# Two FFN-only steps behind the third batch, its loads a step later, and the first output stores issued by SyncE

## The chip, the cores and the metric

One core of a Trainium2 chip. The metric is the time of one execution in microseconds (us) of device time. A core's five engines are called here as the profile calls them: PE is TensorE, ACT is ScalarE, DVE is VectorE, POOL is GpSimd, SP is SyncE. Batches and steps are counted from 0, so the "third batch" of the title is batch 2.

## The reference

Attention over 8 batches of 8 heads, 576 queries of width 64, with 16 extra "beacon" keys ahead of the causal ones; its result goes through a gated FFN.

```python
k_all = np.concatenate([beacon_k, k], axis=2)          # 16 + 576 keys
v_all = np.concatenate([beacon_v, v], axis=2)
scores = scale * np.matmul(q, k_all.transpose(0, 1, 3, 2))
scores = np.where(causal, -1000000000.0, scores)       # future keys; beacons are always seen
a = np.exp(scores - scores.max(-1, keepdims=True))
a /= a.sum(-1, keepdims=True) + 1e-09
x = np.matmul(a, v_all)          # -> (4608 tokens, 512)
gate = np.maximum(x @ w_gate, 0.0)                     # 512 -> 1536
out = gate * (x @ w_val) @ w_out                       # 1536 -> 512
```

## The kernel before

Everything is laid out by hand as a list of steps. A step holds a share of one batch's attention (scores on PE, exp on ScalarE, causal mask on GpSimd, value products on PE, normalisation on VectorE) and some FFN groups of tokens that are finished, so that PE has matmuls while the other engines work. An "up" group is 8 matmuls of 512 columns with a relu and a product; a "down" group is 12 matmuls, a copy and an output store. Integer quotas count groups, the others are us of PE time.

```python
    ALONE = ((0, 3, 3, 2), (4, 4))          # FFN-only steps behind batch 0 and behind batch 1
    ...
    plan = ([(0, i, 0) for i in range(7)]
            + [(None, 0, n) for n in ALONE[0]]
            + [(1, i, 1) for i in range(7)]
            + [(None, 0, n) for n in ALONE[1]]
            + [(2, i, n) for i, n in enumerate((2, 2, 1, 1, 1))]
            + [(b, i, 6.2) for b in range(3, B) for i in range(5)]
            + [(None, 0, 4.5)])
```

From batch 2 on, a batch is brought in by 15 tiles: a load on SyncE's queue, a cast to bf16 on GpSimd some steps later, and for q and k a transposing DMA, again on SyncE's queue, a step after the cast.

```python
        def load(self, x, t, held=False):
            ...
                nc.sync.dma_start(raw[p0:p1].rearrange("p (h d) -> p h d", d=D), ...)
        def turn(self, x, t):
            ...
            nc.sync.dma_start_transpose(dst[:, :, t * P:t * P + n], self.h.pop((x, t))[:n])

        def fetch(b, s0, late=1, held=False):
            at(s0, lambda: batches.update({b: Batch(b)}))
            for j, u in enumerate(LOADS):
                s = s0 + j // 3
                at(s, lambda u=u, h=held and j == 0: batches[b].load(*u, h))
                at(s + late, lambda u=u: batches[b].cast(*u, pool))
                if u[0] != "v":
                    at(s + late + 1, lambda u=u: batches[b].turn(*u))

        fetch(2, s2 + 1, 2, True)                        # s2: the first step of batch 1
        for b in range(3, B):                            # BASE[b]: the first step of batch b
            fetch(b, BASE[b] - (7 if b == 3 else 5), 2 if b == 3 else 1)
```

The store of a down group goes out on one of two queues. The first two FFN tiles (8 stores) use ScalarE's, at once behind the copy. All later ones are put on a list and go out on SyncE's queue at the start of the next step.

```python
                ob = pools["osb"].tile([P, d_model], FP32, name="ob")
                nc.scalar.copy(ob[:, n], o[:, n])
                store = lambda e, m=m, n=n, ob=ob: e.dma_start(out[m:m + P, n], ob[:, n])
                if self.m0 < 2 * M_TILE:
                    store(nc.scalar)
                else:
                    later_sp.append(lambda store=store: store(nc.sync))
    ...
        for s, (b, i, quota) in enumerate(plan):
            acts = later.pop(s, [])           # this step's loads, casts, transposes
            run_sp()                          # the stores on the list
            ...                               # scores, exp, values, FFN groups
            for act_ in acts + later_half.pop(s, []):
                act_()
```

## Time and profile before

| | |
|---|---|
| time before, first three runs | median 395.3 us (394.73 to 400.1) |
| span of the profiled run | 393.6 us |
| PE busy | 371.9 us, so 21.7 us idle |
| the worst stop | 4.15 us before batch 3's first scores, then 3.8 us at clock 0.57 |

The lines behind these figures stand in the prediction and are not shown twice. One listing that is not part of the profile helps to read them: the compiled instruction list of the kernel before, which names the semaphores that each instruction waits for. On ScalarE's and SyncE's queues (row, line, operation, waits):

```
ScalarE
73 L539 TensorCopy ob<-p 128x512 [waits PE_49]
74 L541 DMACopy out_dram<-ob 128x512 [waits DMAHW5_49,Activation_49]
75 L411 Activation e<-p 128x2x3x160 [waits PE_49,Pool_49]
SyncE
82 L250 DMACopy raw<-in_v_dram 128x8x64 [waits DMAHW5_49]
83 L250 DMACopy raw<-in_v_dram 128x8x64 [waits DMAHW6_49]
84 L250 DMACopy raw<-in_v_dram 80x8x64 [waits DMAHW7_49]
85 L275 DmaTransposeAnt kT<-half 128x4x128 [waits DMAHW0_49,Pool_49]
86 L275 DmaTransposeAnt qT<-half 128x4x128 [waits DMAHW1_49,Pool_49]
```

The DMAs of SyncE and ScalarE share eight semaphores, DMAHW0 to DMAHW7, dealt out in the order of the program, and each DMA waits for the one that had its semaphore before. So the fifth store (row 74, with DMAHW5) waits for the v load eight DMAs earlier (row 82, with DMAHW5), on the other queue. That is the wait that the prediction calls a bookkeeping dependence. Call this set the ring.

### The profile page before, as it was taken

Reading aid. Unit: us, or ns where it says so; the run is one execution under the profiler, and the core shown is the slowest. Engines: PE = TensorE matmul, PEld = TensorE weight load, DVE = VectorE, ACT = ScalarE, POOL = GpSimd, SP = SyncE. Lnnn points to the kernel's source line nnn. Section 1 sums busy time; section 2 is a strip of 40 time slices with the busy share of each in tenths; the row PEclk is TensorE's granted clock in tenths of the full one; section 3 lists DMA queues with packets and bytes.
Section 4 is the critical chain, followed back from the end, with each engine's and each line's share of the span. In section 5 each row is a group of like instructions: output and inputs, shape, how many; then the busy total and the mean of one; then the engine's idle time right before and its main releaser. Section 6 shows DMA issues by size and latency. Waiting matters only on the chain.

```text
span 393.6 us, 10209 instructions
## 1 busy us (share of the span) xinstructions
PE 371.9 (94%) x4297; PEld 190.1 (48%) x4297; DVE 198.3 (50%) x309; ACT 191.0 (49%) x272; POOL 123.3 (31%) x219
## 2 busy tenths in 40 slices
PE   6889998989959999999999999999999999999995
PEld 2564544434535555555555555455545544444443
DVE  4768566342633466336742675257525665412420
ACT  3783583238625654575347544655455513323321
POOL 1696654235531523242424252324320200000000
PEclk9999999999998999999999999999999999999999
DMA  7999999799698665597558854985310011002002
GB/s 208 220 213 181 192 198 230 159 194 190 137 193 190 151 127 108 134 208 152 108 134 185 160 115 125 198 139 123 87 55 2 2 56 53 2 36 74 0 28 85
DMA packets 149220, 50.70 MB, mean 129 GB/s; under 512 B 133680, under 2 KB 144688, under 8 KB 149168
## 3 DMA queue, kind: packets, MB, share of 16 engines
q1 hardware_dynamic: 138960, 42.91, 50.5%
q0 software_dynamic: 9056, 4.98, 9.4%
q10 hardware_dynamic: 1152, 2.10, 1.8%
q8 instruction: 35, 0.57, 0.7%
q14 instruction: 17, 0.14, 0.1%
HBM read 38.34 MB, written 9.44 MB: 121 GB/s over the span
## 4 chain that ended last, share of the span: by engine, by line
PE 70%; DMA 16%; SPq 3%; POOL 3%; DVE 2%; ACT 2%; issue 2%; ACTq 0%; DVEq 0%; POOLq 0%
PE p L536 20%; PE p L517 19%; PE p L526 19%; PE p L466 6%; DMA raw<-in_v_dram 4%; DMA wv<-in_moe_w_val_dram 4%; DMA raw<-in_q_dram 3%; DMA raw<-in_k_dram 2%; PE p L403 2%; ACT e L411 2%; DVE hT L528 2%; SPq L250 1%; DMA wide<-in_k_dram 1%; SPq L275 1%; DMA hwide<-in_k_dram 1%
## 5 line engine op out<-in xcount | busy, mean ns | idle before, releaser
L528 DVE TENSOR_TENSOR hT<-g,p 128x512 bf16<-128x512 f32 x89 | 60.7, 684 | 101.2 <-PE p L526 66.9
L419 POOL TENSOR_SCALAR_AFFINE_SELECT e<-e 128x512 bf16<-128x512 bf16 (+2 forms) x80 | 45.7, 592 | 158.8 <-ACT e L411 158.7
L526 PE MATMUL p<-xT,wv 128*128 128x512 bf16 x356 | 91.3, 379 | 0.4 <-ACT e L411 0.4
L517 PE MATMUL p<-xT,wg 128*128 128x512 bf16 x356 | 91.5, 379 | 0.2
L520 ACT ACTIVATE g<-p 128x512 f32<-128x512 f32 x89 | 52.8, 603 | 71.3 <-PE p L517 71.3
L536 PE MATMUL p<-wo,hT 128*128 128x512 bf16 (+1 forms) x396 | 85.5, 373 | 0.2 <-ACT e L411 0.2
L411 ACT ACTIVATE e<-p 128x1024 bf16<-128x1024 f32 (+2 forms) x84 | 75.1, 966 | 21.0 <-PE p L403 12.2
L479 DVE RECIPROCAL r<-p 128x256 f32<-128x256 f32 (+1 forms) x24 | 47.0, 1958 | 43.3 <-PE p L466 43.3
L526 PEld LDWEIGHTS <-wv 128*128 128x128 bf16 x432 | 42.0, 98 | 53.0 <-issue 1.8
L536 PEld LDWEIGHTS <-hT 128*128 128x128 bf16 x444 | 42.1, 98 | 48.2 <-issue 0.5
L517 PEld LDWEIGHTS <-wg 128*128 128x128 bf16 x432 | 40.3, 98 | 49.8 <-issue 3.2
L539 ACT COPY ob<-p 128x512 f32<-128x512 f32 (+1 forms) x33 | 18.9, 573 | 63.5 <-PE p L536 63.5
L270 POOL CAST half<-raw 128x512 bf16<-128x512 f32 (+2 forms) x60 | 35.4, 614 | 17.8 <-DMA raw<-in_q_dram 10.1
L466 PEld LDWEIGHTS <-v 128*32 128x32 bf16 (+1 forms) x1408 | 28.6, 99 | 11.0 <-issue 5.3
L403 PEld LDWEIGHTS <-kT 64*128 64x128 bf16 x704 | 21.0, 97 | 25.6 <-issue 21.1
L466 PE MATMUL p<-e,v 128*32 128x80 bf16 (+4 forms) x1056 | 30.2, 235 | 1.5 <-DVE hT L528 1.0
L411 ACT ACTIVATE e<-s 128x1024 bf16<-128x1024 f32 (+2 forms) x28 | 25.6, 966 | 8.3 <-PE s L403 4.8
L403 PE MATMUL p<-qT,kT 64*128 64x80 bf16 (+3 forms) x528 | 23.3, 230 | 4.8 <-ACT e L411 4.4
L265 POOL CAST v<-raw 128x512 bf16<-128x512 f32 (+1 forms) x38 | 24.0, 656 | 7.6 <-DMA raw<-in_v_dram 7.5
L466 PE MATMUL p<-e,ones 128*32 128x80 bf16 (+4 forms) x528 | 25.0, 234 | 0.0
L517 PE MATMUL f<-xT,wg 128*128 128x512 bf16 x76 | 19.7, 379 | 2.0 <-ACT g L520 1.7
L466 PEld LDWEIGHTS <-ones 128*32 128x32 bf16 (+1 forms) x704 | 19.7, 100 | 0.1
(83 smaller groups left out, 228.3 us busy)
## 6 DMA issues: line engine op xcount, KB each, us to landing
out_dram<-ob SPq DMA_DIRECT2D x27, 256.0 KB, 2.2
raw<-in_q_dram SPq DMA_DIRECT2D x25, 256.0 KB, 5.0
raw<-in_v_dram SPq DMA_DIRECT2D x24, 256.0 KB, 4.1
raw<-in_k_dram SPq DMA_DIRECT2D x19, 256.0 KB, 5.0
out_dram<-ob ACTq DMA_DIRECT2D x8, 256.0 KB, 3.1
raw<-in_v_dram SPq DMA_DIRECT2D x8, 224.0 KB, 3.6
wo<-in_moe_w_out_dram POOLq DMA_DIRECT2D x2, 768.0 KB, 11.9
raw<-in_k_dram SPq DMA_DIRECT2D x6, 224.0 KB, 4.6
```

The costliest lines, as they stand in the source:

```text
L265: copy(self.v[:n, t].rearrange("p (h a d) -> p h a d", a=2, d=C), raw[:n].rearrange("p (h d a) -> p h a d", a=2, d=C))
L270: copy(h[:n], raw[:n])
L403: nc.tensor.matmul(self.s[:, a, c + j * n:c + (j + 1) * n], kT[rows, 2 * g + j, k0:k0 + P], qT[rows, 2 * g + j, q0:q0 + n], start=True, st ...
L411: nc.scalar.activation(e[:, :k * 4 * n].rearrange("p (k a x) -> p a k x", k=k, a=2), self.s[:, :, :k * 2 * n].rearrange("p a (k x) -> p a ...
L419: nc.gpsimd.affine_select(out=cols[:, :, :m], in_=cols[:, :, :m], pattern=[[0, 4], [1, m]], compare_op=ALU.is_ge, fill=0.0, base=base, cha ...
L466: nc.tensor.matmul(o[:, q0 - cq0:q0 - cq0 + n], w, e[:kr, 2 * (hh % 2) + hh // 2], start=(x == 0 and i == 0 and part != 1), stop=stop, ski ...
L479: nc.vector.reciprocal(self.r[:, :self.n], self.os[:, :self.n])
L517: nc.tensor.matmul(g[:, :n], wg[:, ki, nf * P:(nf + 1) * P], x[:, ki], start=(ki == 0), stop=(ki == KM - 1))
L520: nc.scalar.activation(gs[:, :n], g[:, :n], AF.Relu)
L526: nc.tensor.matmul(u[:, :n], wv[:, ki, nf * P:(nf + 1) * P], x[:, ki], start=(ki == 0), stop=(ki == KM - 1))
L528: nc.vector.tensor_mul(self.h[:, nf, c0:c1], gs[:, :n], u[:, :n])
L536: nc.tensor.matmul(o[:, n], self.h[:, nf, ms * P:(ms + 1) * P], wo[:, nf, n], start=(nf == 0), stop=(nf == NF - 1))
```

## The change

Its intent: SyncE is one to two steps late at batches 2 and 3, and its lateness reaches PE in two ways, through the transposed tiles and through ScalarE's queue. The change gives batch 3 more time (part B: two FFN-only steps in front of it, paid for by its own quota), lets batch 2's loads start a step later (part C, whose casts stay two steps behind), and takes the stores off ScalarE (part A), behind each step's loads and transposes.

```diff
-                store = lambda e, m=m, n=n, ob=ob: e.dma_start(out[m:m + P, n], ob[:, n])     # A
-                if self.m0 < 2 * M_TILE:
-                    store(nc.scalar)
-                else:
-                    later_sp.append(lambda store=store: store(nc.sync))
+                later_sp.append(
+                    lambda m=m, n=n, ob=ob: nc.sync.dma_start(out[m:m + P, n], ob[:, n]))
 ...
-    ALONE = ((0, 3, 3, 2), (4, 4))
+    ALONE = ((0, 3, 3, 2), (4, 4), (2, 3))                                                    # B
 ...
-            + [(b, i, 6.2) for b in range(3, B) for i in range(5)]
+            + [(None, 0, n) for n in ALONE[2]]
+            + [(b, i, 4.1 if b == 3 else 6.2) for b in range(3, B) for i in range(5)]
 ...
-        fetch(2, s2 + 1, 2, True)
+        fetch(2, s2 + 2, 2, True)                                                             # C
 ...
             acts = later.pop(s, [])
+            behind_acts = later_sp[:] if s < BASE[3] else []                                  # A
+            if behind_acts:
+                later_sp.clear()
             run_sp()
 ...
-            for act_ in acts + later_half.pop(s, []):
+            for act_ in acts + later_half.pop(s, []) + behind_acts:
                 act_()
```

(One effect of B is not in the diff's text: BASE[3] grows by two, so batch 3's loads are planned for step 20 and not 18.)

## The prediction

> **What bounds the kernel now.** I read the page first: the engine totals and the row of forty slices.
>
> ```profile
> span 393.6 us, 10209 instructions
> ...
> PE 371.9 (94%) x4297; PEld 190.1 (48%) x4297; DVE 198.3 (50%) x309; ACT 191.0 (49%) x272; POOL 123.3 (31%) x219
> ...
> PE   6889998989959999999999999999999999999995
> ...
> PEclk9999999999998999999999999999999999999999
> ```
>
> TensorE is the bound: it is idle for only 393.6 - 371.9 = 21.7 us. The change adds and removes no matmul, so it can win only idle time, and time in which the clock was low. One slice in the middle stands out (the twelfth, a 5), and the clock dips right after it. Then I took busy times by stretches. From 60 to 131 us PE is busy 62.19 of 71.0 us (8.8 idle); from 131 to 389 us it is busy 256.55 of 258 (1.45 idle in all). The rest of the idle time, some 11.5 us, lies before 60 us and in the last 5 us, where the diff changes nothing. So the whole prize is in 60 to 131 us. Around the bad slice the columns are window, length, busy time of PE, PEld, DVE, ACT, POOL, granted clock, DMA share, GB/s:
>
> ```profile
> 109.34:112.10 2.76, 2.76 (x20) 1.08 (x12) 2.60 (x3) 0.00 (x0) 1.07 (x2) 1.00 1.40 118
> 112.10:116.26 4.16, 0.01 (x2) 0.09 (x2) 0.51 (x2) 1.02 (x2) 0.00 (x0) 1.00 1.06 195
> 116.26:120.08 3.82, 3.47 (x96) 2.60 (x96) 0.10 (x1) 2.09 (x4) 2.23 (x4) 0.57 0.74 194
> ```
>
> A stop of 4.16 us, then 3.82 us at a clock of 0.57. The timeline of PE (start, length, what; in brackets the idle time before it and its releaser) shows what ended this stop, and an earlier one:
>
> ```profile
> 80.62 1.02 PE L517 MATMUL f<-xT,wg 128*128 128x512 bf16 x4 [1.69 <-ACT g L520]
> ...
> 116.26 0.40 PE L403 MATMUL p<-qT,kT 64*128 64x256 bf16 x4 [4.15 <-ACT e L411]
> ```
>
> Both times ScalarE was late, though it is busy only half the time. Its own timeline says why:
>
> ```profile
> 79.53 0.34 ACTq L541 DMA_DIRECT2D out_dram<-ob  x1
> 79.97 1.08 ACT L520 ACTIVATE g<-f 128x512 f32<-128x512 f32 x2 [3.87 <-DMA raw<-in_v_dram]
> ...
> 107.62 0.59 ACT L539 COPY ob<-p 128x512 f32<-128x512 f32 x1 [2.05 <-PE p L536]
> 114.79 0.34 ACTq L541 DMA_DIRECT2D out_dram<-ob  x1
> 115.23 1.56 ACT L411 ACTIVATE e<-p 128x960 bf16<-128x960 f32 x2 [7.03 <-DMA raw<-in_v_dram]
> ```
>
> ScalarE finished the copy at 108.2, then its queue stood at the output store until 114.79. The store needed only that copy, yet the chain of waits releases it by the landing of a v load, issued at 111.17 and landed at 114.72. So it waited on a bookkeeping dependence on another DMA that comes a little earlier in the program and that SyncE issued late. At 79.53 it is the same (a v load landed at 79.46). I read the last view, SyncE's timeline, for why it is late: between 68.8 and 118.6 us it has hardly a gap.
>
> ```profile
> 87.38 1.20 SPq L275 DMA_TRANSPOSE qT<-half  x1
> 88.64 0.58 SPq L250 DMA_DIRECT2D raw<-in_beacon_k_dram  x1
> ...
> 111.17 2.20 SPq L250 DMA_DIRECT2D raw<-in_v_dram  x3
> ```
>
> Batch 3 (counting from 0) has its loads planned for step 18, which PE ran at 72 to 82 us. SyncE issued them from 88.64: it runs a step or two behind the plan. Its 15 loads and 10 transposes took until 118.6, while PE wanted batch 3 at 112.1.
>
> **What the Trainium skill says.** "TensorE: Matmul & The Clock Gate", Part 1 (the HAM clock gate): the clock falls to half after an idle window of about 3.4 us and comes back after about 3.4 us of work. The trace agrees: 4.16 us idle, then 0.57 over 3.82 us, and the gap of 1.69 us at 80 us brought no such dip. "DMA: Bandwidth & Descriptors", anatomy of one DMA: a semaphore wait of a DMA happens on the issuing sequencer before dispatch, not on the DMA engines. The trace agrees: ScalarE's queue stood from 108.2 to 114.79. The same page, "Issuing engines are not separate DMA queues": all issuers share 16 engines, a second issuer saves only issue time. So moving the 8 stores costs no bandwidth; what it costs is SyncE's issue time, 0.34 us each here. "Perfetto Trace Analysis", What "DMA-bound" means: a DMA-bound stretch may be bound by the issuing sequencer, with solid DMA slices on its track. SyncE at 69 to 118 us looks like that.
>
> **The change part by part.**
> 1. Stores of the first two FFN tiles (8 of them) go from ScalarE to SyncE, one step later, behind that step's transposes and loads. ScalarE no longer stands behind SyncE. This frees the 1.69 us gap, and the ScalarE side of the 4.15 us gap.
> 2. Two FFN-only steps (2 and 3 groups) before batch 3. By the quotas and the trace these hold two down groups of tile 1 (2.65 us each, as 5.29 for 24 matmuls) and three up groups of tile 2 (1.73 each): 10.5 us, plus the last value products of batch 2 (1.2), moved from batch 3's first step. Batch 3's quota falls from 6.2 to 4.1, 5 x 2.1 = 10.5. I followed the credits: before, batch 3's five steps do 12 ups and 4 downs; after, the seven steps do the same. Nothing is added on PE. But batch 3 is wanted 11.7 us later, and its loads (planned two steps later, now step 20) start later only as far as SyncE is late.
> 3. Batch 2's loads one step later. The GpSimd memset that holds them back falls at about 55 us instead of 51.95. The DMA engines are full from 40 to 68 us (share 0.99 or more), so most of the 3 us is hidden: weights come sooner, these loads end about as before. GpSimd's casts stand one step further behind the masks.
>
> Won, from PE's timeline:
> - the stop before batch 3: 4.15 + 0.20 + 0.15 (gaps at 116.26, 116.85, 120.08) = 4.5
> - the low clock: the 84 value products took 2.1 us there and 1.13 at 103.69; the score products 1.36 (without the gap) against 0.86: 1.5
> - the gap at 80.62: 1.7
> - gaps at 68.64 (0.94, a mask queued on GpSimd behind a cast that waited for a load), 60.81 (0.23, w_out late), 71.78 (0.15): 1.3
> - the gap at 127.56 (0.39, exp late): 0.4
> Sum 9.4 us.
>
> Given back:
> - Batch 2's last transpose (q tile 4) was issued at 87.38; with a landing of 2.5 it is there at 89.9. Now three stores go ahead of it (0.34 + 0.1 between issues = 1.3) and I take 0.5 from the later loads: 91.7. PE would want it at the second step of batch 2, at 93.81 - 3.0 (the gaps up to there) = 90.8. Stall 0.9.
> - Batch 3's steps are shorter (6 us against 8), so small waits at step boundaries (0.16 to 0.43 us in this trace) show a little more: 0.6, a choice.
> Net 9.4 - 1.5 = 7.9. From 395.3: 387.4 us.
>
> Is SyncE in time for batch 3? Shifted by 3 us (1.8 as above and some stores) its last transpose goes from 117.37 to about 121 and lands at 123.5. PE's first step of batch 3 comes at 112.1 - 2 + 11.7 = 122 and needs tiles turned at 109.5, now about 113, landed 116; its second step, at 126, needs the last one. Some 3 to 6 us of room. Batch 4 then has 30 us instead of 40 for the same 15 loads and 10 transposes; these took SyncE 30 us in its crowded stretch and some 25 us of issue time else, and batch 4's last-needed transpose has about 3 us to spare.
>
> **The rivals.**
> (a) SyncE stays the bound: the stall only moves to batch 2's or batch 4's start. For it: solid slices from 69 to 118, and PE comes earlier while SyncE gets more to issue. Against: 11.7 us of other work put in front of batch 3. If a stop of 2 to 4 us remained, with the clock dip where it exceeds the window, the time would be 390 to 393.
> (b) The stores alone are the gain, the two steps idle decoration. Against: PE's weight load for batch 3's first scores waited for a transpose until 112.81 in any case, and with 3 us won earlier PE would wait there for nearly 4 us. I expect both parts needed; the time of the whole would be the same.
> (c) Everything idle between 60 and 131 us goes: 8.8 + 1.5 = 10.3, so 385.
> (d) The shorter steps of batch 3 make ScalarE the limit: per step up to 3 exps (0.97) and 3 relus (0.60), 4.7 us of about 6, so near but under; if it bound, 1 to 2 us lost, 389.
>
> **Range and chances.** The mechanism is well carried by the trace; the size lies right at the 2% line (387.4). Full success gives 385, a partly moved stall 390. Range 385.3 to 390.4. Faster by over 2%: 0.47; within 2%: 0.51; slower: 0.02.
>
> **What would show it.** The twelfth slice of PE at 9 and no low clock after 30 us; ScalarE with no queue entry of the store; its first store-free copy followed at once by an exp; PE idle from 60 to 131 us of 1 to 3 us; after 131 us still about 1.5. PE busy total 1.5 us less. I am wrong if PE shows a new stop at batch 2's first steps or at batch 3's or 4's start, ended by a transpose (kT or qT from half), or if idle time appears in the seven steps from 112 to 152.

## The result, and the profile after

| | before | after |
|---|---|---|
| median time | 395.95 us (4 runs, 394.73 to 400.1) | 385.25 us (4 runs, 385.14 to 385.93) |
| span of the profiled run | 393.6 us | 384.0 us |
| PE busy / idle in it | 371.9 / 21.7 us | 370.1 / 13.9 us |

The ratio is 0.9715, with a 95% interval of 0.9653 to 0.9777: faster. Here and below a ratio is the mean time of one kernel's runs over that of the other's of the same rounds, so it is not quite the ratio of the medians that are quoted. The prediction was 387.4 with a range from 385.3: the median lies 0.05 us under the range. Repeated later, with more rounds beside new runs of the kernel before, the ratio was 0.9746 (0.9719 to 0.9772).

The page of the kernel after: span, busy times, PE's forty slices and its clock.

```profile
span 384.0 us, 10206 instructions
...
PE 370.1 (96%) x4297; PEld 189.3 (49%) x4297; DVE 200.0 (52%) x309; ACT 191.1 (50%) x272; POOL 123.4 (32%) x219
...
PE   7989999999999999999999999999999999999995
...
PEclk9999999999999999999999999999999999999999
```

The slice with a 5 in the middle is gone, and so is the dip of the clock behind it. The stretches, first of the kernel before (window, length, busy PE, PEld, DVE, ACT, POOL, clock, DMA share, GB/s):

```profile
60.00:131.00 71.00, 62.19 (x805) 32.27 (x804) 31.60 (x48) 33.50 (x46) 29.32 (x52) 0.98 0.91 184
131.00:375.00 244.00, 242.70 (x2651) 122.63 (x2650) 124.90 (x178) 116.58 (x168) 59.01 (x106) 1.00 0.45 100
```

Then of the kernel after:

```profile
60.00:131.00 71.00, 69.90 (x855) 35.39 (x855) 38.21 (x57) 37.09 (x53) 29.89 (x52) 1.00 0.96 185
131.00:375.00 244.00, 242.56 (x2651) 122.72 (x2651) 122.27 (x171) 115.39 (x166) 58.76 (x105) 1.00 0.48 100
```

PE's idle time in the first stretch fell from 8.8 us (71.0 - 62.19) to 1.1 (71.0 - 69.90); in the second it is what it was (1.3 and 1.4). The whole gain lies where the prediction looked. PE's timeline after, at the second step of batch 2, at the largest gap that is left between 60 and 160 us, and at the first step of batch 3:

```profile
90.35 0.82 PE L403 MATMUL p<-qT,kT 64*128 64x128 bf16 x24
...
99.64 0.60 PE L403 MATMUL p<-qT,kT 64*128 64x128 bf16 x12 [0.43 <-DVE xT L495]
...
120.29 0.83 PE L403 MATMUL p<-qT,kT 64*128 64x256 bf16 x12
```

The first and the last have no bracket: PE did not wait for batch 2's last transpose, nor for batch 3. On ScalarE the store-free copy is followed at once by an exp. The line before had an idle time of 7.03 us in this place:

```profile
104.17 0.59 ACT L539 COPY ob<-p 128x512 f32<-128x512 f32 x1 [2.05 <-PE p L536]
104.65 1.57 ACT L411 ACTIVATE e<-p 128x960 bf16<-128x960 f32 x2
```

SyncE's timeline is needed for the step of the prediction that failed. First the kernel before, where batch 2's transposes begin (they end with the issue at 87.38 that the prediction shows):

```profile
68.82 1.31 SPq L275 DMA_TRANSPOSE kT<-half  x1
```

Then the kernel after, the first and the last of these transposes with the stores around the last:

```profile
67.56 1.38 SPq L275 DMA_TRANSPOSE kT<-half  x1
...
86.75 0.53 SPq L542 DMA_DIRECT2D out_dram<-ob  x1
87.37 1.20 SPq L275 DMA_TRANSPOSE qT<-half  x1
88.67 0.52 SPq L542 DMA_DIRECT2D out_dram<-ob  x1
```

The last transpose, which I had expected 1.8 us later, was issued at the same time as before (87.37 and 87.38). It landed 2.3 us later, at 89.7, by the answer for this one transpose:

```profile
DMA to landing us min/median/max: 2.3/2.3/2.3
```

PE came at 90.35. The stretch from the first transpose's start to the last one's end did grow, from 19.76 us (88.58 - 68.82) to 21.01 (88.57 - 67.56), with three stores of 1.56 us together in it. But it began 1.26 us earlier.

### The profile page after: what moved, and what is told of

The parts are those of the page before.

```text
span 384.0 us, 10206 instructions
## 1 busy us (share of the span) xinstructions
PE 370.1 (96%) x4297; PEld 189.3 (49%) x4297; DVE 200.0 (52%) x309; ACT 191.1 (50%) x272; POOL 123.4 (32%) x219
## 4 chain that ended last, share of the span: by engine, by line
PE 87%; DVE 6%; DMA 3%; issue 1%; ACT 1%; POOL 1%; SPq 0%; DVEq 0%
PE p L536 21%; PE p L517 20%; PE p L526 19%; PE p L466 8%; PE f L517 4%; DVE hT L528 3%; PE f L536 3%; PE p L403 2%; PE s L526 2%; PE s L403 2%; DVE r L479 2%; DMA wv<-in_moe_w_val_dram 2%; PE f L526 2%; PE ab L466 1%; DMA wide<-in_k_dram 1%
## 5 line engine op out<-in xcount | busy, mean ns | idle before, releaser
L466 PEld LDWEIGHTS <-v 128*32 128x32 bf16 (+1 forms) x1408 | 27.8, 98 | 9.7 <-issue 4.2
L466 PE MATMUL p<-e,v 128*32 128x80 bf16 (+4 forms) x1056 | 29.3, 231 | 1.6 <-DVE hT L528 1.0
L466 PE MATMUL p<-e,ones 128*32 128x80 bf16 (+4 forms) x528 | 24.2, 230 | 0.0
```

The lines of the kernel that those rows point to most:

```text
L466: nc.tensor.matmul(o[:, q0 - cq0:q0 - cq0 + n], w, e[:kr, 2 * (hh % 2) + hh // 2], start=(x == 0 and i == 0 and part != 1), stop=stop, ski ...
```

## The experiments

Theory: the stop had two independent releasers, ScalarE standing at its stores (through the ring) and SyncE's late transposes, so A and B pay only together, and C saves the small gap behind a mask. Rivals: SyncE is the bound, so any version moves the stop; or the stores alone, or the steps alone, are the gain. All three parts and their pairs were run, then variants of each part. Every kernel was timed in rounds with the kernel before on the same chip, except the last four. All outputs are right.

| kernel | parts | median us | ratio to before (95%) |
|---|---|---|---|
| only_stores | A | 392.5 | 0.9931 (0.9868 to 0.9994) |
| only_steps | B | 396.55 | 1.0004 (0.9922 to 1.0086) |
| only_late | C | 391.81 | 0.9908 (0.9816 to 0.9999) |
| no_late | A, B | 385.94 | 0.9768 (0.9737 to 0.9799) |
| no_late_again | A, B | 387.55 | 0.9794 (0.9766 to 0.9822) |
| no_steps | A, C | 391.24 | 0.9916 (0.9878 to 0.9954) |
| no_steps_19 | A, C, batch 3 loaded later | 392.49 | 0.9904 (0.9833 to 0.9974) |
| no_stores | B, C | 394.38 | 0.9982 (0.9950 to 1.0013) |
| after_again | A, B, C | 385.46 | 0.9746 (0.9719 to 0.9772) |
| stores_front | A, B, C, stores ahead of the transposes | 385.25 | 0.9723 (0.9657 to 0.9789) |
| stores_pool | B, C, stores on GpSimd | 384.96 | 0.9747 (0.9718 to 0.9775) |
| stores_halved | A, B, C, each early store in two | 389.71 | 0.9873 (0.9834 to 0.9911) |

### One part taken away

**no_stores** (the stores back on ScalarE):

```diff
-                later_sp.append(
-                    lambda m=m, n=n, ob=ob: nc.sync.dma_start(out[m:m + P, n], ob[:, n]))
+                store = lambda e, m=m, n=n, ob=ob: e.dma_start(out[m:m + P, n], ob[:, n])
+                if self.m0 < 2 * M_TILE:
+                    store(nc.scalar)
+                else:
+                    later_sp.append(lambda store=store: store(nc.sync))
```

> The changed kernel with the first eight stores on ScalarE's queue again. Theory: ScalarE stands again at each store until SyncE has issued and landed the DMA eight earlier in the program; the gap at 80 us comes back (1.7) and the stores of tile 1 block exp and relu in steps 24 to 26, where PE stops 3 us or more in all: 390 to 394. Rival 'slack before batch 3 is the whole gain': 386 to 388.

Measured: 394.38 us, ratio 0.9982. Without A, the two other parts gain nothing that the interval shows. ScalarE's timeline and PE's:

```profile
121.56 0.36 ACTq L541 DMA_DIRECT2D out_dram<-ob  x1
122.02 0.59 ACT L539 COPY ob<-p 128x512 f32<-128x512 f32 x1 [6.48 <-DMA qT<-half]
```

```profile
122.66 1.70 PE L526 MATMUL p<-xT,wv 128*128 128x512 bf16 x4 [2.56 <-ACT ob L539]
...
125.81 1.87 PE L517 MATMUL p<-xT,wg 128*128 128x512 bf16 x4 [1.46 <-ACT g L520]
```

ScalarE stood 6.48 us at a store, released by the landing of a transpose, a DMA of the other queue that has nothing to do with the store's data. In the FFN-only steps the store stands between the copy and the relus that PE waits for, so PE stops twice. The clock in the 2 us windows from 122 us on:

```profile
122.00:124.00 2.00, 1.34 (x4) 0.53 (x4) 0.00 (x0) 0.59 (x1) 0.00 (x0) 0.72 0.63 181
124.00:126.00 2.00, 0.54 (x2) 0.10 (x1) 0.21 (x1) 0.84 (x2) 0.00 (x0) 0.50 0.98 221
126.00:128.00 2.00, 2.00 (x6) 0.69 (x5) 1.88 (x4) 0.54 (x2) 0.00 (x0) 0.50 1.18 269
```

The stops also lowered the clock to 0.50.

**no_steps** (the FFN-only steps and the lower quota out):

```diff
-    ALONE = ((0, 3, 3, 2), (4, 4), (2, 3))
+    ALONE = ((0, 3, 3, 2), (4, 4))
-            + [(None, 0, n) for n in ALONE[2]]
-            + [(b, i, 4.1 if b == 3 else 6.2) for b in range(3, B) for i in range(5)]
+            + [(b, i, 6.2) for b in range(3, B) for i in range(5)]
```

> The changed kernel without the two FFN-only steps (quota 6.2 again). Two causes in series: PE wants batch 3 at about 108.7 us, the transposes it needs land near 112.5: a stop of 3.5 to 5 us plus 1.5 us of low clock, perhaps one more at the second step of batch 3; 390 to 392. Rival 'the stores are the whole gain': 385 to 386.5.

Measured: 391.24 us, ratio 0.9916: the expected time, but the stop came in another place than expected, at batch 2's second step and hardly at batch 3's first (0.48 us):

```profile
94.38 0.58 PE L403 MATMUL p<-qT,kT 64*128 64x80 bf16 x12 [3.89 <-DMA qT<-half]
```

SyncE's timeline shows why. With C and without B, batch 3's loads are planned for the step in which batch 2's last transpose stands, and are ahead of it:

```profile
87.27 0.57 SPq L250 DMA_DIRECT2D raw<-in_beacon_k_dram  x1
...
89.64 1.07 SPq L542 DMA_DIRECT2D out_dram<-ob  x1
90.80 1.20 SPq L275 DMA_TRANSPOSE qT<-half  x1
```

So the FFN-only steps do two things: they put work ahead of batch 3, and through BASE[3] they move batch 3's loads behind batch 2's transposes. **no_steps_19** separates the two. It has no FFN-only steps, but batch 3's loads a step later:

```diff
-            fetch(b, BASE[b] - (7 if b == 3 else 5), 2 if b == 3 else 1)
+            fetch(b, BASE[b] - (6 if b == 3 else 5), 2 if b == 3 else 1)      # on top of no_steps
```

> In the run without the FFN-only steps the stop came 15 us earlier than I had said, at batch 2's second step, because there batch 3's first loads were planned a step ahead of batch 2's last transpose and stood before it on SyncE. Here batch 3's loads are planned a step later, so that order is as in the changed kernel. If the FFN-only steps are needed because SyncE is late for batch 3, the stop of 3.5 to 5 us is now at batch 3's first step (PE wants it near 108.7 us; the transposes land near 112.5), ended by a transpose, with low clock after it: 389.5 to 392. If it was only the order, the time falls to 385 to 387.

Measured: 392.49 us, ratio 0.9904, the same as no_steps within the intervals. The stop is back at batch 3's first step:

```profile
114.14 0.83 PE L403 MATMUL p<-qT,kT 64*128 64x256 bf16 x12 [2.33 <-DMA qT<-half]
```

The order of the loads only chooses which batch waits. What removes the stop is other work for PE while SyncE catches up. (This profiled run also waited 2.6 us for a weight at 51 and 53 us, which put PE later and so probably made this stop shorter.)

**no_late** and **no_late_again** (batch 2's loads at the step of before):

```diff
-        fetch(2, s2 + 2, 2, True)
+        fetch(2, s2 + 1, 2, True)
```

> The changed kernel with batch 2's loads a step earlier again. Theory: the gaps of 0.94 (mask behind a cast), 0.23 (w_out late) and 0.15 us come back, and SyncE reaches batch 2's last transpose about 2 us later (three stores ahead of it and no quicker loads), so PE may wait up to 1 us at batch 2's second step: 386.5 to 387.5. Rival 'the later loads do nothing': 385.3.

> The changed kernel with batch 2's loads a step earlier, a second time and with more rounds. In its first run PE showed two gaps of 0.27 and 0.44 us behind masks that the changed kernel doesn't have, and the last transpose of batch 2 was issued no later (87.1 us). Theory 'the later loads are worth these gaps': 0.5 to 0.9 us above the changed kernel, on this chip. Rival 'they do nothing': within 0.2 us.

Measured: ratios 0.9768 and, with five rounds, 0.9794 against 0.9746 for the kernel after in the same call. By the medians part C is worth 2 us, about half a per cent, where I had put 1.3 us on it; but the two intervals still touch, so its worth is not settled. The later last transpose that I had expected in no_late did not come: it was issued at 87.08 us, against 87.37 in the kernel after. In the profiled run of no_late_again (389.84 us, slow beside its median of 387.55) the mask gap cost more than its length; PE's timeline, then the window behind the gap:

```profile
70.24 0.26 PE L466 MATMUL ab<-e,v 80*32 80x80 bf16 x8 [1.71 <-POOL e L419]
```

```profile
70.20:74.00 3.80, 3.60 (x20) 1.44 (x21) 2.22 (x4) 0.00 (x0) 2.36 (x4) 0.57 0.54 109
```

A stop of 1.71 us, with some light work ahead of it, was followed by 3.8 us at 0.57. In the first run of the same kernel the gap was 0.44 us. The mask's lateness differed this much between two profiles of one kernel, so what C is worth probably varies from run to run.

### One part alone

**only_stores** (A alone):

> The stores alone move to SyncE; no FFN-only steps, loads of batch 2 as before. Theory 'two causes in series' (ScalarE stood behind SyncE through the store; SyncE itself is late for batch 3): ScalarE is freed and the 1.7 us gap at 80 us goes, but PE then arrives some 2 us earlier at batch 3 and waits there for a transpose, which in the kernel before was only there at 112.8 us: a stop of 3 to 5 us at 110 us, ended by a transpose and not by exp, clock low after it. Time 391 to 394. Rival 'the stores are the whole gain': no stop, 385 to 387.

Measured: 392.5 us, ratio 0.9931, as expected. PE's timeline, and the windows of the stop and behind it:

```profile
113.43 1.46 PE L403 MATMUL p<-qT,kT 64*128 64x256 bf16 x12 [4.68 <-DMA qT<-half]
```

```profile
108.70:113.40 4.70, 0.06 (x1) 0.00 (x0) 0.98 (x2) 0.58 (x1) 2.38 (x4) 0.99 0.91 179
113.40:118.00 4.60, 4.57 (x102) 3.25 (x103) 1.03 (x1) 2.85 (x3) 1.74 (x3) 0.64 1.07 210
```

The stop at batch 3 is even longer than before (4.68 against 4.15 us), and its releaser is now a transposed tile and no longer ScalarE's exp. This is the second releaser, which the exp had hidden. That rules out rival (b) of the prediction.

**only_steps** (B alone):

> The FFN-only steps alone. ScalarE's stores still wait in the ring with SyncE's DMAs, also in the FFN-only steps, where each of their copies is followed by such a store: 393.5 to 396, as in the kernel before. If slack before batch 3 were worth something by itself: 389 to 392.

Measured: 396.55 us, ratio 1.0004. No gain: ScalarE stands at its stores in the new steps (it was idle for 5.14 us before its copy at 122.53, until a transpose had landed), and PE's timeline has two new stops:

```profile
123.17 1.02 PE L526 MATMUL p<-xT,wv 128*128 128x512 bf16 x4 [1.22 <-ACT ob L539]
...
126.71 1.02 PE L517 MATMUL p<-xT,wg 128*128 128x512 bf16 x4 [2.52 <-ACT g L520]
```

The first was released by ScalarE's copy, the second by its relu. A mask gap of 2.60 us at 69.77, longer than in the kernel before (0.94), cost this profiled run besides. That rules out the rival that the steps alone are the gain.

**only_late** (C alone):

> The later loads of batch 2 alone. The gap behind a mask near 68 us (0.94) goes; PE then waits as much longer at batch 3's start: 393 to 396, within 1 us of the kernel before.

Measured: 391.81 us, ratio 0.9908: better than I expected. The mask gap is gone, and PE still stops at 79.05 (2.03 us, relu), 93.84 (1.01, transpose) and 113.72 (2.05, transpose). The stop at batch 3 is half of before's, but two more stand behind it, 0.87 us at 122.63 (released by ScalarE's copy) and 1.46 at 124.90 (by its exp). With these PE was idle as long between 60 and 131 us as in the kernel before (9.0 us against 8.8); what this run lacked is the low clock. So C alone did not mend the stop, and why its time is better stays open. C alone gives 0.92%, C on top of A and B some 0.5%, but the first interval reaches 0.9999, so whether parts of the gain are shared is not shown.

### Where and how the stores go

**after_again** (the kernel after, unchanged):

> The changed kernel again, to set the next three against it on one chip: 385.0 to 385.6.

Measured: 385.46 us, ratio 0.9746. Its profiled run was its slowest (388.55), with a lower clock in the first 30 us.

**stores_front** (the stores ahead of the step's transposes instead of behind):

```diff
-            behind_acts = later_sp[:] if s < BASE[3] else []
-            if behind_acts:
-                later_sp.clear()
+            behind_acts = []
```

> The changed kernel with each step's stores ahead of that step's transposes and loads instead of behind them. One more store (0.6 us) stands ahead of batch 2's last transpose, which landed 1.1 us before PE needed it: within 0.5 us of the changed kernel (385 to 386). If the place behind the transposes matters, over 1 us slower, with a PE wait ended by a transpose.

Measured: 385.25 us, ratio 0.9723, not to be told from the kernel after. One small gap came with it, because the last transpose stands behind one more store:

```profile
90.56 0.39 PE L403 MATMUL p<-qT,kT 64*128 64x80 bf16 x12 [0.25 <-DMA qT<-half]
```

In this profile the place behind the transposes is worth that, 0.25 us.

**stores_pool** (the eight stores issued by GpSimd):

```diff
-                    lambda m=m, n=n, ob=ob: nc.sync.dma_start(out[m:m + P, n], ob[:, n]))
+                    lambda m=m, n=n, ob=ob: (nc.gpsimd if m < 2 * M_TILE else nc.sync).dma_start(
+                        out[m:m + P, n], ob[:, n]))
```

> The changed kernel with the first eight stores on GpSimd's queue, which takes its DMA semaphores from another set, so neither ScalarE nor SyncE shares anything with them. If what counts is that ScalarE doesn't wait in SyncE's ring of eight semaphores, this is as fast as the changed kernel: 385.0 to 385.8, ScalarE without a stop, and SyncE issues batch 2's last transpose some 2 us earlier (about 85.5 us), as four stores of 0.5 us leave its stretch. If SyncE as the issuer matters for itself (order behind the transposes), it is slower by over 1 us.

Measured: 384.96 us, ratio 0.9747, equal to the kernel after. Batch 2's last transpose was issued at 86.81, 0.6 us earlier than in the first profile of the kernel after; I had expected nearly 2. (In after_again it was issued at 89.34, but that run was late from its start.) What matters is that the stores leave ScalarE, not that SyncE takes them. GpSimd's DMAs have semaphores of their own in the instruction list (DMASW).

**stores_halved** (each of the eight stores as two, to double their issue time on SyncE):

```diff
-                later_sp.append(
-                    lambda m=m, n=n, ob=ob: nc.sync.dma_start(out[m:m + P, n], ob[:, n]))
+                for h in ((slice(0, 256), slice(256, 512)) if self.m0 < 2 * M_TILE else (n,)):
+                    later_sp.append(
+                        lambda m=m, h=h, ob=ob: nc.sync.dma_start(out[m:m + P, h], ob[:, h]))
```

> The changed kernel with each of the first eight stores issued as two of half the width, so SyncE issues eight more. Three more issues of 0.6 us stand ahead of batch 2's last transpose (87.4 us, landed 89.7, needed by PE at 90.8). If SyncE's issue time is what my prediction took it for, this transpose lands at about 91.6 and PE waits 0.7 to 1.2 us there: 0.5 to 1.3 us above the changed kernel. If waits for semaphores pace SyncE and issues fit in between, it stays within 0.2 us.

Measured: 389.71 us, ratio 0.9873, some 4 us slower than the kernel after, where I had expected about 1. In the profiled run batch 2 did not stop. The delay was carried on to the batch that I had not looked at:

```profile
160.76 0.39 PE L403 MATMUL p<-qT,kT 64*128 64x80 bf16 x12 [1.35 <-DMA qT<-half]
```

That is batch 4's second step. It accounts for 1.35 us; this run also had a low clock at its start, as the profiled run of after_again had (388.55 us), and the rest of the 4 us between the medians is not traced to a place. The same wait stands, shorter, in four other profiles of kernels with parts B and C: 0.50 us in after_3, 0.31 and 0.33 in the two of stores_pool, 0.42 in no_stores_2. So SyncE has little or no room up to batch 4. Whether the eight more issues or the shorter rows of the halved stores were too much was not separated.

### Did leaving ScalarE bring SyncE forward?

After these runs it was open why batch 2's transposes began earlier in the kernel after. One theory: stores on ScalarE take part in the ring, so SyncE's DMAs also wait for them. The other: scatter between runs. The last four runs repeat kernels from above, with no edit.

> Stores on ScalarE, loads late, FFN-only steps: a second profile for the time of batch 2's first transpose on SyncE. If ScalarE's stores in the shared ring hold SyncE back: 68.5 to 70 us (first profile 69.8). If the difference is scatter: anywhere from 66 to 70.

> The changed kernel, a third profile: first transpose of batch 2 at 67.0 to 68.0 us (67.56 and 67.51 so far) if the ring theory holds; scatter theory: 66 to 70.

> As for the second profile of this kernel: 68.5 to 70 us under the ring theory, 66 to 70 under scatter.

> Stores on GpSimd, outside the ring: 67 to 68.2 us under the ring theory (67.97 so far), 66 to 70 under scatter.

Measured: 393.63, 386.09, 392.6 and 385.69 us (one run each, beside 397.48 for before). The first transpose of batch 2 started at 68.65, 67.06, 67.81 and 67.18 us. Three of the four fell where the ring theory put them, no_stores_3 did not. Over all profiles, the first transpose started on average at 68.6 us where the stores are ScalarE's (6 profiles, 67.8 to 69.8) and at 67.5 where they are not (12 profiles, 65.7 to 69.0). The means differ by 1.1 us in the direction of the theory, but the ranges overlap, and no profile shows a wait of a SyncE load released by a store of ScalarE. The instruction lists settle one part. In all four kernels with these stores on ScalarE (before, no_stores, only_steps, only_late), no DMA on SyncE's queue up to batch 2's first transpose takes a semaphore that a store of ScalarE had before it; the first one that does is a load behind the third transpose. So the ring cannot have delayed this first transpose directly, and the ring theory falls as it was put.

A rival that no run tests is the traffic of the stores. A store moves 262 kB (128 x 512 x 4 bytes). In the six profiles with stores on ScalarE the first one goes out at 62.2 to 63.6 us, ahead of the first transpose, while batch 2's loads are under way; in the twelve others it goes out behind that transpose, but for stores_front (68.11 against 68.59). At the 196 to 279 GB/s that the kernel before moved between 62 and 68 us, I estimate one store at 0.9 to 1.3 us of the DMA engines' time, which is about the difference. The cause of the earlier start stays open. That ScalarE is held back by SyncE through the ring is shown by the 6.48 us above.

## Why the prediction was right or wrong

**The bound and the place: right.** All of the gain came between 60 and 131 us; idle time there fell to 1.1 us, and after 131 us it stayed at 1.4.

**Won: right in size.** Predicted were 7.9 us of idle time (4.5 + 1.7 + 1.3 + 0.4) and 1.5 of low clock, 9.4 in all. Measured were 7.8 us less idle (21.7 - 13.9) and 1.8 less busy (371.9 - 370.1), 9.6 in all, the whole difference of the two spans (393.6 - 384.0).

**Both parts needed: right, and shown.** A alone 0.993, B alone 1.000, A with B 0.977 to 0.979. A single part leaves the other releaser of the stop in place: the transposed tile in only_stores, ScalarE behind its store in only_steps and no_stores. Rival (b) fell.

**Given back: this step failed.** It put "Stall 0.9" at batch 2's second step and "0.6, a choice" on the small gaps of shorter steps, 1.5 us together. The profile after shows neither. The stall was worked out as the last transpose there at 91.7 against PE at 90.8. It was there at 89.7 against PE at 90.35, so the 0.9 us of stall is 0.7 us of room. (The two later profiles of this kernel show no stall there either.) The transpose landed 2.0 us earlier than predicted: 1.76 us from its start (1.26 early instead of 0.5 late), 0.2 from the landing (2.3 us instead of 2.5), the rest from the stretch. PE came 0.45 us earlier than predicted, which took that much back. The two terms, by the profile:

- "Three stores ... 1.3": the sum came out by luck. The stretch of the transposes grew by 1.25 us, but the three issues took 1.56 us and some 0.1 us between issues each, together near 1.9, and the rest of the stretch was 0.6 shorter (its third transpose took 1.20 us instead of 2.52).
- "I take 0.5 from the later loads": the first transpose was not late but 1.26 us early, though its loads started 3.4 us later (55.44 against 52.06). Among the profiles without stores on ScalarE, those with the late loads begin 0.4 us later than those with the early ones (67.6 over nine, 67.2 over three), and among those with such stores there is no difference (68.6 over four, 68.7 over two). So the 0.5 was about right or a little high, and it was outweighed by something I had not put in the sum: with the stores off ScalarE the transposes start earlier, by 1.1 us on average. Its cause is the point left open above.
- The "0.6, a choice": the gaps left between 60 and 160 us are of 0.16 and 0.43 us, of the kinds that were there before. Nothing was added, and idle time after 131 us rose by only 0.1.

The sum of the error: by the spans, 1.5 us given back too much and 0.2 won too little. The times of the two profiled runs (395.34 and 385.93) differ by 0.2 less than their spans, and the median after lies 0.7 below its profiled run: 1.5 + 0.2 - 0.2 + 0.7 = 2.2, the distance from 387.4 to 385.25. Rival (c), "everything idle between 60 and 131 us goes", at 385, came nearest (1.1 us stayed idle there), and the lower end of the range cut it off by 0.3. A range that names a rival should hold it.

**Rivals (a) and (d).** In the first profile of the kernel after the stall did not move to batch 2 or 4, but rival (a) was close: no_steps has the stop at batch 2 (3.89 us), stores_halved at batch 4 (1.35), and after_3, the same kernel as after, has 0.50 us at batch 4's second step. The "3 us to spare" that the prediction gave batch 4 were not there in that run. ScalarE did not become the bound in batch 3's shorter steps: no gap of that kind is in PE's timeline.

**Part C.** Its 1.3 us may be right (some 2 by the medians, with intervals that touch), but the mask gap was 0.44 and 1.71 us in two profiles of the same kernel, and behind the second the clock was low. Its single value was the reading of one trace.

## What to carry to other kernels

In this kernel a store on ScalarE's queue put ScalarE behind everything that the store waited for (idle for 7.03 us before one exp), and that included an unrelated DMA of another queue through a shared set of semaphores: look at what releases a store before you put it between a copy and an exp. When a stop has two releasers, removing either one shows little (0.7% and nothing here, 2.1 to 2.3% for both); in thought, take away the one that the trace names, and ask what would have ended the stop next. When a range is drawn, include the rival in which everything goes well, unless the profile speaks against it.

## What the Trainium skill lacked or had wrong

- "TensorE: Matmul & The Clock Gate", Part 1 (the HAM clock gate): an idle window of about 3.4 us lowers the clock. Long stops agree (4.16 us gave 0.57; 4.68 gave 0.64), but shorter ones did it too: 1.71 us was followed by 0.57 over 3.8 us in no_late_again, and 2.56 us by 0.50 in no_stores, while 2.03 and 2.05 us in only_late brought no dip. The page calls the window free-running, and by these stops the length of one stop alone does not decide: staying under 3.4 us was not enough here.
- "DMA: Bandwidth & Descriptors", Issuing engines are not separate DMA queues: a second issuer saves only issue time. Here a second issuer also costs: with the eight stores on ScalarE the ratio to before is 0.9982, on SyncE 0.9746, on GpSimd 0.9747, and ScalarE stood up to 6.48 us at one store. I found no page that tells of DMAs on two queues coupled through a program's reuse of a small set of DMA semaphores (eight here).
- "Perfetto Trace Analysis", DMA Optimizations: it says that one issuing engine for inputs and another for outputs may make sense, especially with loops or control flow. In this kernel that separation between SyncE and ScalarE for the first eight stores was the harm, by the same numbers; with GpSimd for them it was neither better nor worse than SyncE for all.
- The issue times that this argument needed come from the trace: on SyncE 1.20 us for most transposes of a 128x512 tile and 0.50 to 0.53 us for its stores in the crowded stretch, where ScalarE's took 0.34 to 0.38 (I had reckoned with 0.34 for SyncE too), and 0.54 to 0.60 for the same stores on GpSimd. I found no such times by engine for this chip in "DMA: Bandwidth & Descriptors", where they belong.
